# Tiles moved to multiples of 512 bytes, keys and values padded to five full pieces, five matmuls on zeros ahead of the first keys

## The chip, the cores and the metric

The kernel runs on one core of one Trainium2 chip. The metric is the device time of one execution in microseconds (us), the median over several runs.

## The reference

Linear attention over 4 batches of 576 tokens with 8 heads of 64, a normalisation, and then two gated layers of the same shape (512 to 1536 to 512) on all 2304 tokens, in float32:

```python
kv = np.einsum('bhsd,bhse->bhde', k, v)
out = np.einsum('bhsd,bhde->bhse', q, kv)
out = out / np.sqrt(np.mean(out * out, axis=-1, keepdims=True) + 1e-06) * g_norm
x = out.transpose(0, 2, 1, 3).reshape(2304, 512)
x = (x @ w_a) * (x @ w_b) @ w_out                       # first layer
x = 1.0 / (1.0 + np.exp(-(x @ w_gate))) * (x @ w_val) @ w_out2   # second layer
```

## The kernel before

**The layers.** Both layers are worked in twelve rounds: two layers (m) by six quarters of the hidden width (q). A round has three groups, one for each token tile j, whose two halves hold 256, 384 or 512 tokens (`NB`). The 512 by 512 blocks of a group are multiplied with seven block products instead of eight (names "1" to "7", in the order of `SLOTS`), each for the two hidden blocks u and v. Every operand is split into a high and a low part, so one block product is six matmuls: two slices of the contraction by high-high, high-low and low-high (line 724, in `product`). The stationary operand is a tile `wp0` to `wp3` with the weights ("1" and "2" use `wp0`, "5" and "7" use `wp1`, "6" and "4" use `wp2`, "3" uses `wp3`), the moving operand lies in `area0` or `area1`. The projection back to 512 ("down", line 837) uses `wo` and the gated values `gu`, `gv`. In the first round of a layer the moving operands are made on the chip (`x_comb`, line 477 and its neighbours) and stored to DRAM (line 481); in the later rounds they are loaded from there (line 496).

One round thus has 252 product matmuls (84 of each length; of the 84, 24 each on `wp0`, `wp1`, `wp2` and 12 on `wp3`) and 120 down matmuls (72 of 512 columns, 48 of 384).

**The attention.** `keys_values(b)` loads a batch's keys and values in four pieces (one for two heads), multiplies them with float32 matmuls of 128 columns (line 563), and ACT copies the diagonal blocks into `kvbd`. 576 rows are 4.5 times 128: four products use 128 partitions, and the fifth uses 64 partitions of a further piece `rest`, which holds the end of all four and is loaded first. Keys of batch 0 go to the arena, those of later batches to parts of `part0` to `part2` that are not yet in use (`PLACES`). Queries follow per token tile (line 639), then the squares, the mean and the root on ACT, DVE and POOL, a transpose on TensorE (line 674) and a copy into `part`. A float32 matmul leaves two records in the trace, a transposing one leaves one.

**The order.** A planner (`Plan.order`) plays the program with estimated costs and due times and writes one fixed order for every engine; the table `SHIFT` moves single due times. All DMAs are issued by SP, in that order: an issue that waits holds those behind it. Raw weights (line 345) are loaded into a ring of two buffers. Such a buffer is free once ACT (lines 354, 358) and DVE (`sign`, line 370) have read it.

**Places in SBUF.** Tiles are laid one after another, each rounded up to 32 bytes of a partition. `ident` has 512 bytes; `gcol` and `warm` have one word each, the two `ss`, the one `root` and the two `rr` buffers 96 bytes each. In the built program the tiles behind them start at these remainders of 512: `part0` to `part2` 160, both areas 192, `wp0` 192, `wp3` 384, `wp1`, `wp2`, `wo`, `gu` and `gv` 160. Offsets inside the tiles that line 724 and line 837 use are multiples of 512.

Of the kernel before, what the change touches and what calls it, by code (L numbers as in the profile page):

```python
# [23 lines left out]
P = 128  # L24
KC = DM // P
# [8 lines left out]
KJ = 4  # L34
LAST = S - KJ * P
# [19 lines left out]

STARTS = (24000, 50000, 75000)

SHIFT = {
# [26 lines left out]
}  # L85
ANY_ORDER = ("o0", "o1")
ARENA = ("xr",)
# [150 lines left out]
def attention_then_two_moes(  # L238
# [17 lines left out]
    gcol = one.tile([P, 1], F32, name="gcol")  # L256
# [15 lines left out]
    def new_tile(tag, shape, dtype=F32):  # L272
        if tag in ATTENTION:
            lo, n = ATTENTION[tag][0], int(np.prod(shape))
            i = turns[tag] = (turns.get(tag, -1) + 1) % RINGS.get(tag, 1)
            t = area(0)[:, lo + i * n:lo + (i + 1) * n]
            return t if len(shape) == 1 else t.rearrange("p (a b) -> p a b", a=shape[0])
# [34 lines left out]
    def mms(n):  # L312
        return 6 * (n / 2.4 + 9.5 + n / 90)
# [20 lines left out]
    FIRST = [("load", (0, c)) for c in "ab"] + [("kv", 0, p) for p in (KC, *range(KC))] + [("q", t) for t in range(4)]  # L334
    FIRST += ["gcol"] + [("load", (1, c)) for c in "ab"]
    FIRST += [("kv", 1, p) for p in (KC, *range(KC))] + [("q", t) for t in range(4, 9)]
    FIRST += [("kv", 2, p) for p in (KC, *range(KC))] + [("q", t) for t in range(9, 12)] + [("kv", 3, p) for p in (KC, *range(KC))]
# [188 lines left out]
    PLACES = [(2, 0, 0), (2, 0, LOADED), (2, 1, 0), (2, 1, LOADED), (1, 0, 0), (1, 1, 0)]  # L526
    PLACE_OF = {1: (0, 1, 2, 3, 4), 2: (5, 0, 1, 2, 3), 3: (0, 1, 2, 0, 3)}
# [6 lines left out]
    def keys_values(b):  # L534
        bank = ("K", b)
        rest = ("kv", b, KC)

        for p in (KC, *range(KC)):
# [373 lines left out]
    with tc.manual_schedule():  # L912
# [6 lines left out]
        for o in done:  # L919
            o["fn"](ENG[o["on"]]) if len(o["eng"]) == 2 else o["fn"]()  # L920
# [35 lines left out]
```

## Time and profile before

| | us |
|---|---|
| median of 3 runs | 934.97 (932.95 to 935.36) |
| the profiled execution, its own time | 928.55 |
| span of the profiled execution, first to last instruction | 926.8 |
| TensorE busy in it | 891.4 (96%) |
| VectorE / ScalarE / GpSimd busy | 626.3 / 404.1 / 417.1 |
| DMA | 255.66 MB, 276 GB/s |

The span and the execution's own time differ by 1.75 us, which lie around the span; the profiled execution was 6.4 us shorter than the median of the others. Busy time says how long an engine had something under way, not that it could not have been faster.

### The profile page before, as it was taken

Reading aid. Unit: us, or ns where it says so; the run is one execution under the profiler, and the core shown is the slowest. Engines: PE = TensorE matmul, PEld = TensorE weight load, DVE = VectorE, ACT = ScalarE, POOL = GpSimd, SP = SyncE. Lnnn points to the kernel's source line nnn. Section 1 sums busy time; section 2 is a strip of 40 time slices with the busy share of each in tenths; the row PEclk is TensorE's granted clock in tenths of the full one; section 3 lists DMA queues with packets and bytes.
Section 4 is the critical chain, followed back from the end, with each engine's and each line's share of the span. In section 5 each row is a group of like instructions: output and inputs, shape, how many; then the busy total and the mean of one; then the engine's idle time right before and its main releaser. Section 6 shows DMA issues by size and latency. Waiting matters only on the chain.

```text
span 926.8 us, 13401 instructions
## 1 busy us (share of the span) xinstructions
PE 891.4 (96%) x4856; PEld 798.5 (86%) x4856; DVE 626.3 (68%) x1082; ACT 404.1 (44%) x761; POOL 417.1 (45%) x387
## 2 busy tenths in 40 slices
PE   6798997999999999999999999999999999999998
PEld 5687886889988989989989988889989889989986
DVE  3577885378768866766769886767767677645445
ACT  3465653334344433343355555445444344333231
POOL 2568743265545415425458873345534414322111
PEclk9799999999999999999999999999999999999999
DMA  8896477988888797787694578798697696587573
GB/s 294 263 313 229 184 260 228 363 322 327 289 325 311 245 370 267 250 346 274 211 376 188 212 294 334 257 349 321 225 370 270 235 346 245 193 318 239 187 278 124
DMA packets 55472, 255.66 MB, mean 276 GB/s; under 512 B 6256, under 2 KB 8304, under 8 KB 44656
## 3 DMA queue, kind: packets, MB, share of 16 engines
q1 hardware_dynamic: 55408, 254.83, 75.0%
q8 instruction: 38, 0.62, 0.3%
q14 instruction: 26, 0.21, 0.1%
HBM read 217.06 MB, written 37.75 MB: 275 GB/s over the span
## 4 chain that ended last, share of the span: by engine, by line
PE 87%; DMA 7%; ACT 2%; DVE 2%; POOL 1%; issue 1%; SPq 0%; ACTq 0%; DVEq 0%; POOLq 0%
PE ps_u L724 53%; PE ps_o L837 29%; DMA raw<-w_all_dram 4%; PE ps_o L563 3%; PE ps_o L639 1%; DMA x<-area 1%; PE ps_o L674 1%; DMA area<-x 1%; DMA part<-kv_in_dram 1%; DMA area<-kv_in_dram 1%; ACT mag L354 0%; POOL wp L422 0%; DVE mag L370 0%; DVE gf L798 0%; POOL w L376 0%
## 5 line engine op out<-in xcount | busy, mean ns | idle before, releaser
L724 PE MATMUL ps_u<-area,wp 128*128 128x256 f32 (+2 forms) x3024 | 556.1, 339 | 13.0 <-DMA area<-x 4.7
L724 PEld LDWEIGHTS ps_u<-area,wp 128*128 128x128 f32 x3024 | 492.7, 189 | 62.9 <-ACT vu L326 5.1
L837 PE MATMUL ps_o<-gu,wo 128*128 128x512 f32 (+1 forms) x720 | 188.9, 370 | 1.8 <-DVE part L851 0.9
L837 PE MATMUL ps_o<-gv,wo 128*128 128x512 f32 (+1 forms) x720 | 187.3, 368 | 0.0
L847 DVE TENSOR_TENSOR part<-ps_o,part 128x512 f32<-128x512 f32 (+1 forms) x200 | 126.6, 635 | 84.0 <-PE ps_o L837 83.1
L376 POOL TENSOR_TENSOR w<-mag,last 128x512 int32<-128x512 int32 x72 | 96.5, 1345 | 127.9 <-DVE mag L370 119.8
L837 PEld LDWEIGHTS ps_o<-gv,wo 128*128 128x128 f32 x720 | 132.7, 188 | 17.6
L837 PEld LDWEIGHTS ps_o<-gu,wo 128*128 128x128 f32 x720 | 129.3, 188 | 19.4 <-DVE part L851 1.4
L806 POOL TENSOR_TENSOR gu<-gf,gu 128x512 fp32r<-128x512 f32 (+2 forms) x50 | 53.1, 1063 | 169.1 <-ACT gu L803 169.0
L354 ACT ACTIVATE mag<-raw 128x512 f32<-128x512 f32 x72 | 48.2, 669 | 75.0 <-DMA raw<-w_all_dram 63.7
L422 POOL TENSOR_TENSOR wp<-tmp,wp 128x512 fp32r<-128x512 f32 x33 | 43.6, 1321 | 75.9 <-ACT wp L418 75.9
L362 DVE TENSOR_SCALAR mag<-mag 128x512 f32<-128x512 f32 x72 | 36.6, 509 | 35.8 <-ACT mag L354 35.7
L803 ACT ACTIVATE gu<-gf 128x256 fp32r<-128x256 f32 (+2 forms) x72 | 37.5, 521 | 43.2 <-DVE gf L798 42.5
L370 DVE SCALAR_TENSOR_TENSOR mag<-raw,mag 128x512 uint32<-128x512 uint32 x72 | 49.4, 687 | 0.8
L418 ACT ACTIVATE wp<-tmp 128x512 fp32r<-128x512 f32 x48 | 30.3, 632 | 42.0 <-PE ps_u L724 34.2
L422 POOL TENSOR_TENSOR wp<-w,wp 128x256 fp32r<-128x256 f32 (+1 forms) x30 | 29.7, 991 | 41.8 <-ACT wp L418 41.6
L418 ACT ACTIVATE wp<-w 128x512 fp32r<-128x512 f32 (+1 forms) x48 | 25.2, 525 | 52.2 <-PE ps_u L724 41.3
L358 ACT ACTIVATE last<-raw 128x512 int32<-128x512 uint32 x72 | 47.5, 663 | 0.0
L326 ACT ACTIVATE u2u<-ps_u 128x512 f32<-128x512 f32 (+2 forms) x34 | 16.8, 494 | 69.3 <-PE ps_u L724 69.3
L806 POOL TENSOR_TENSOR gv<-gf,gv 128x384 fp32r<-128x384 f32 (+2 forms) x30 | 31.3, 1044 | 28.5 <-ACT gv L803 28.1
L803 ACT ACTIVATE gv<-gf 128x256 fp32r<-128x256 f32 (+2 forms) x72 | 37.7, 523 | 13.3 <-DVE gf L798 11.2
L806 DVE TENSOR_TENSOR gv<-gf,gv 128x256 fp32r<-128x256 f32 (+2 forms) x42 | 37.0, 880 | 8.9 <-ACT gv L803 8.9
(88 smaller groups left out, 892.6 us busy)
## 6 DMA issues: line engine op xcount, KB each, us to landing
area<-x SPq DMA_DIRECT2D x70, 1024.0 KB, 6.8
area<-x SPq DMA_DIRECT2D x70, 768.0 KB, 5.5
raw<-w_all_dram SPq DMA_DIRECT2D x72, 512.0 KB, 5.7
area<-x SPq DMA_DIRECT2D x70, 512.0 KB, 5.8
x<-area SPq DMA_DIRECT2D x14, 1024.0 KB, 4.7
x<-area SPq DMA_DIRECT2D x14, 768.0 KB, 3.3
x<-area SPq DMA_DIRECT2D x14, 512.0 KB, 4.0
part<-kv_in_dram SPq DMA_DIRECT2D x12, 512.0 KB, 5.7
```

The source lines that it names most:

```text
L354: A.activation(out=tl["mag", k], in_=words(1).bitcast(F32), func=ACTF.Abs, scale=65536.0)
L358: A.activation(out=tl["last", k], in_=words(0), func=ACTF.Copy, scale=2.0**-29)
L362: V.tensor_scalar(out=m, in0=m, scalar1=LEAST, scalar2=MOST, op0=ALU.max, op1=ALU.min)
L370: V.scalar_tensor_tensor(out=m, in0=words(1), scalar=0x80000000, in1=m, op0=ALU.bitwise_and, op1=ALU.bitwise_or)
L376: G.tensor_tensor(out=tl["w32", k].bitcast(I32), in0=tl["mag", k].bitcast(I32), in1=tl["last", k], op=ALU.add)
L418: A.activation(out=tl[name][:, 0, :], in_=tl[src][:, cut], func=ACTF.Copy)
L422: eng.tensor_tensor(out=t[:, 1, :], in0=tl[src][:, cut], in1=t[:, 0, :], op=ALU.subtract)
L724: nc.tensor.matmul(out=o, lhsT=wt[:, a, c], rhs=x[:, b, k, :], start=(i in "152" and k == 0 and (a, b) == (0, 0)), stop=(k == 1 and (a, b) ...
L803: A.activation(out=tl[whole][:, 0, c], in_=tl[me, "gf", t], func=ACTF.Copy)
L806: eng.tensor_tensor(out=tl[whole][:, 1, c], in0=tl[me, "gf", t], in1=tl[whole][:, 0, c], op=ALU.subtract)
L837: nc.tensor.matmul(out=o[:, :N], lhsT=tl["wo", f_of(g, uv)][:, a, c], rhs=tl[rhs["uv".index(uv)]][:, b, :], start=(uv, a, b) == ab[0], sto ...
L847: V.tensor_tensor(out=acc, in0=o, in1=acc, op=ALU.add)
```

## The change

Five edits. The small tiles (`gcol`, `warm`, `ss`, `root`, `rr`) become slices of one tile `small` of 896 bytes, so that in the built program every tile behind it starts at a multiple of 512 bytes. Keys and values are padded with zero rows from 576 to 640, so that a batch has four pieces of five times 128 rows and no `rest`; there are five places for them. Five float32 matmuls of 512 columns on the zeroed `kvbd[1]` stand ahead of everything else on TensorE. The planner's cost of six matmuls has another formula. `SHIFT` is another table.

```diff
-KJ = 4
-LAST = S - KJ * P
+KJ = 5
+HEAT = 5
...
 ANY_ORDER = ("o0", "o1")
+SMALL = {"ss": 32, "root": 32 + 6 * H, "rr": 32 + 9 * H}
+SMALL_WORDS = 224
...
     ident = one.tile([P, P], F32, name="ident")
-    gcol = one.tile([P, 1], F32, name="gcol")
+    small = one.tile([P, SMALL_WORDS], F32, name="small")
+    gcol, warm = small[:, 0:1], small[:, 1:2]
...
     def new_tile(tag, shape, dtype=F32):
+        if tag in SMALL:
+            i = turns[tag] = (turns.get(tag, -1) + 1) % RINGS.get(tag, 1)
+            t = small[:, SMALL[tag] + i * 3 * H:SMALL[tag] + (i + 1) * 3 * H]
+            return t if len(shape) == 1 else t.rearrange("p (a h) -> p a h", a=3)
...
     def mms(n):
-        return 6 * (n / 2.4 + 9.5 + n / 90)
+        return 6 * (n + 16 * -(-n // 256)) / 2.4
...
-    PLACES = [(2, 0, 0), (2, 0, LOADED), (2, 1, 0), (2, 1, LOADED), (1, 0, 0), (1, 1, 0)]
-    PLACE_OF = {1: (0, 1, 2, 3, 4), 2: (5, 0, 1, 2, 3), 3: (0, 1, 2, 0, 3)}
+    PLACES = [(2, 0), (2, LOADED), (2, 2 * LOADED), (1, 0), (1, LOADED)]
+    PLACE_OF = {1: (0, 1, 2, 3), 2: (4, 0, 1, 2), 3: (0, 1, 2, 0)}
...
-                for j, t in enumerate([tl[kv][:, j] for j in range(KJ)] + [tl[rest][:, p]]):
-                    nc.tensor.matmul(out=tl[bank][:, p, :], lhsT=t[:, 0, :], rhs=t[:, 1, :], start=(j == 0), stop=(j == KJ))
+                t = tl[kv]
+                for j in range(KJ):
+                    nc.tensor.matmul(
+                        out=tl[bank][:, p, :], lhsT=t[:, j, 0, :], rhs=t[:, j, 1, :], start=(j == 0), stop=(j == KJ - 1)
+                    )
...
         V.memset(kvbd[1], 0.0)
         G.memset(kvbd[0], 0.0)
+        hot = bank_of("o0")
+        for _ in range(HEAT):
+            nc.tensor.matmul(out=hot, lhsT=kvbd[1][:, 0, :], rhs=kvbd[1].rearrange("p k n -> p (k n)"), start=True, stop=True)
...
-    kv_in = np.zeros((B, KC + 1, P, KJ, 2, P), np.float32)
-    kv_in[:, :KC] = kv[:, :, :KJ * P].reshape(B, KC, P, KJ, 2, P)
-    kv_in[:, KC, :LAST] = kv[:, :, KJ * P:].transpose(0, 2, 1, 3, 4)
-    kv_in = kv_in.reshape(B, KC + 1, P, KJ * 2 * P)
+    kv_in = np.zeros((B, KC, P * KJ, 2, P), np.float32)
+    kv_in[:, :, :S] = kv
+    kv_in = kv_in.reshape(B, KC, P, KJ * 2 * P)
```

The start of TensorE's order, before: keys of batch 0 (`area_92`), queries of the first four token tiles (`ps_u`), keys of batch 1 (`part_67`, and `part_66` for the `rest`).

```order
L563 MATMUL ps_o_115<-area_92 128x128 x20
L639 MATMUL ps_u_151<-area_71,part_65 128x128 x4
L639 MATMUL ps_u_160<-area_71,part_65 128x128 x4
L639 MATMUL ps_u_167<-area_71,part_65 128x128 x4
L639 MATMUL ps_u_194<-area_71,part_65 128x128 x4
L563 MATMUL ps_o_221<-part_67 128x128 x4
L563 MATMUL ps_o_221<-part_66 128x128
```

The same place in the changed kernel:

```order
L932 MATMUL ps_o_82<-area_71 128x512 x5
L573 MATMUL ps_o_125<-area_98 128x128 x20
L650 MATMUL ps_u_191<-area_71,part_65 128x128 x4
L650 MATMUL ps_u_197<-area_71,part_65 128x128 x4
L650 MATMUL ps_u_205<-area_71,part_65 128x128 x4
L650 MATMUL ps_u_219<-area_71,part_65 128x128 x4
L573 MATMUL ps_o_241<-part_67 128x128 x15
L573 MATMUL ps_o_241<-part_66 128x128 x5
```

The five matmuls on zeros stand first; what follows has kept its order, with three pieces of batch 1 in `part_67` and one in `part_66`.

The start of SP's order of DMA issues, before: raw weights (`raw`), queries (`part_65`, `area_71`), keys and values of batch 0 (`area_92`) and batch 1 (`part_66`, `part_67`).

```order
L345 DMA raw<-w_all_dram 128x512
L632 DMA part_65<-q_t_dram 128x512
L556 DMA area_92<-kv_in_dram 64x1024
L556 DMA area_92<-kv_in_dram 128x1024 x4
L632 DMA part_65<-q_t_dram 128x512 x2
L345 DMA raw<-w_all_dram 128x512 x2
L556 DMA part_66<-kv_in_dram 64x1024
L556 DMA part_67<-kv_in_dram 128x1024
L632 DMA part_65<-q_t_dram 128x512
L556 DMA part_67<-kv_in_dram 128x1024
L345 DMA raw<-w_all_dram 128x512
L865 DMA gcol<-g_col_dram 128x1
```

In the changed kernel:

```order
L357 DMA raw<-w_all_dram 128x512 x2
L565 DMA area_98<-kv_in_dram 128x1280 x4
L643 DMA part_65<-q_t_dram 128x512 x3
L357 DMA raw<-w_all_dram 128x512
L565 DMA part_67<-kv_in_dram 128x1280
L643 DMA part_65<-q_t_dram 128x512
L357 DMA raw<-w_all_dram 128x512
L565 DMA part_67<-kv_in_dram 128x1280
L877 DMA small<-g_col_dram 128x1
L565 DMA part_67<-kv_in_dram 128x1280
L565 DMA part_66<-kv_in_dram 128x1280
```

Two raw loads now stand ahead of the first keys, each piece of keys is 640 KB instead of 512 KB, and the last piece of batch 1 stands behind the fourth raw load, as two of its pieces did before.

## Rows read from the trace of the kernel before

**Rows 1.** The page: the span, busy time of each engine.
```profile
span 926.8 us, 13401 instructions
...
PE 891.4 (96%) x4856; PEld 798.5 (86%) x4856; DVE 626.3 (68%) x1082; ACT 404.1 (44%) x761; POOL 417.1 (45%) x387
```

**Rows 2.** Stretches: length, then each engine's busy us, granted clock, DMA share, GB/s.
```profile
core 0: us, PE busy (x) PEld busy (x) DVE busy (x) ACT busy (x) POOL busy (x), PEclk, DMA share, GB/s
0.00:5.00 5.00, 0.00 (x0) 0.00 (x0) 0.79 (x2) 2.48 (x4) 1.18 (x8) 1.00 0.63 210
...
10.00:15.00 5.00, 5.00 (x23) 4.09 (x21) 0.00 (x0) 0.00 (x0) 0.00 (x0) 1.00 1.05 391
...
20.00:25.00 5.00, 4.06 (x32) 3.50 (x30) 4.42 (x9) 3.10 (x7) 3.76 (x8) 1.00 0.69 133
...
30.00:35.00 5.00, 4.14 (x16) 3.07 (x16) 1.29 (x2) 0.76 (x2) 2.77 (x4) 0.50 0.59 202
...
40.00:50.00 10.00, 9.14 (x68) 8.03 (x67) 8.15 (x16) 6.80 (x15) 5.79 (x10) 1.00 0.92 312
...
200.00:923.00 723.00, 719.21 (x3864) 647.85 (x3862) 497.69 (x864) 303.27 (x573) 311.29 (x259) 1.00 0.76 279
```

**Rows 3.** The same view, inside and over one steady round.
```profile
289.35:290.78 1.43, 1.43 (x13) 1.42 (x12) 1.43 (x3) 0.71 (x2) 1.43 (x3) 1.00 0.72 221
290.78:292.19 1.41, 1.41 (x14) 1.41 (x13) 0.76 (x2) 1.24 (x3) 1.41 (x2) 1.00 0.89 259
308.81:310.17 1.36, 1.36 (x14) 1.36 (x12) 1.36 (x4) 0.78 (x2) 1.25 (x2) 1.00 0.68 262
...
312.25:314.37 2.12, 2.12 (x13) 2.12 (x13) 1.92 (x3) 2.10 (x5) 2.12 (x2) 1.00 0.87 294
330.34:333.10 2.76, 2.76 (x13) 2.25 (x13) 2.56 (x6) 1.42 (x3) 1.05 (x2) 1.00 0.87 289
335.89:338.62 2.73, 2.73 (x13) 2.25 (x12) 0.69 (x1) 0.63 (x1) 0.46 (x1) 1.00 1.01 402
286.61:355.41 68.80, 68.80 (x374) 62.22 (x374) 51.30 (x93) 29.23 (x54) 30.09 (x28) 1.00 0.84 308
```

**Rows 4.** Timeline of TensorE in that round: start, us, engine, line, operation.
```profile
338.62 0.68 PE L837 MATMUL ps_o<-gu,wo 128*128 128x384 f32 x3
...
340.70 2.96 PE L724 MATMUL ps_u<-area,wp 128*128 128x512 f32 x12
343.50 0.70 PE L837 MATMUL ps_o<-gu,wo 128*128 128x384 f32 x3
```

**Rows 5.** Timeline, the first 41 us.
```profile
0.89 0.48 DVE L917 MEMSET area<- 128x512 f32 x1 [0.89 <-PEq L945]
...
7.50 9.04 PE L563 MATMUL ps_o<-area 128*128 128x128 f32 x40 [7.50 <-DMA area<-kv_in_dram]
...
40.31 1.57 PE L563 MATMUL ps_o<-part 128*128 128x128 f32 x10
```

**Rows 6.** Chain that ended last, in order of time, the first 34 us.
```profile
19.84 0.69 DVE mag L370
...
20.59 0.33 SPq L345
...
21.44 6.14 DMA part<-kv_in_dram
...
27.62 5.49 PE ps_o L563 x20
```

**Rows 7.** The same chain from 142 us on.
```profile
143.06 9.35 DMA x<-area
...
152.79 6.68 DMA area<-x
```

**Rows 8.** Who waited for whom: engine, line, releaser, us, times, longest.
```profile
PE ps_u L724 <- DMA area<-x: 4.7, 4, 2.4
...
PE ps_o L563 <- DMA part<-kv_in_dram: 3.6, 1, 3.6
```

More of the change, by code (lines that the diff above doesn't have):

```diff
@@ L330, in move @@
             eng.tensor_scalar(out=out, in0=in_, scalar1=scale, scalar2=None, op0=ALU.mult)
-    FIRST = [("load", (0, c)) for c in "ab"] + [("kv", 0, p) for p in (KC, *range(KC))] + [("q", t) for t in range(4)]
+    FIRST = [("load", (0, c)) for c in "ab"] + [("kv", 0, p) for p in range(KC)] + [("q", t) for t in range(4)]
     FIRST += ["gcol"] + [("load", (1, c)) for c in "ab"]
-    FIRST += [("kv", 1, p) for p in (KC, *range(KC))] + [("q", t) for t in range(4, 9)]
-    FIRST += [("kv", 2, p) for p in (KC, *range(KC))] + [("q", t) for t in range(9, 12)] + [("kv", 3, p) for p in (KC, *range(KC))]
+    FIRST += [("kv", 1, p) for p in range(KC)] + [("q", t) for t in range(4, 9)]
+    FIRST += [("kv", 2, p) for p in range(KC)] + [("q", t) for t in range(9, 12)] + [("kv", 3, p) for p in range(KC)]
     load_due = {name: 100 * i - 1e5 for i, name in enumerate(FIRST)}
@@ L535, in keys_values @@
         bank = ("K", b)
-        rest = ("kv", b, KC)
-        for p in (KC, *range(KC)):
+        for p in range(KC):
             kv = ("kv", b, p)
@@ L545, in keys_values @@
                 before, new, uses = last_in.get(place, []), [], []
-                last_in[place] = [("K", b, x) for x in (range(KC) if p == KC else (p,))]
+                last_in[place] = [("K", b, p)]
             def load(p=p, kv=kv):
-                rows = P if p < KC else LAST
                 if b == 0:
@@ L552, in load @@
                 else:
-                    j, h, lo = PLACES[PLACE_OF[b][p]]
-                    t = part[j][:, h].rearrange("p k n -> p (k n)")[:, lo:lo + LOADED]
-                t = t[:rows]
-                nc.sync.dma_start(out=t, in_=kv_in[b, p, :rows])
+                    j, lo = PLACES[PLACE_OF[b][p]]
+                    t = part[j].rearrange("p h k n -> p (h k n)")[:, lo:lo + LOADED]
+                nc.sync.dma_start(out=t, in_=kv_in[b, p])
                 tl[kv] = t.rearrange("p (j c e) -> p j c e", c=2, e=P)
@@ L561, in mm @@
                     tl[bank] = bank_of("o1").rearrange("p (k n) -> p k n", k=KC)
-                for j, t in enumerate([tl[kv][:, j] for j in range(KJ)] + [tl[rest][:, p]]):
-                    nc.tensor.matmul(out=tl[bank][:, p, :], lhsT=t[:, 0, :], rhs=t[:, 1, :], start=(j == 0), stop=(j == KJ))
-            op(kv, "SP", dma(512 if p < KC else 256), load, before, new, rank=load_due[kv], lag=2000)
-            if p < KC:
-                op(("K", b, p), "PE", 1130, mm, [kv, rest] + ([("K", b, p - 1)] if p else [("O", t) for t in tiles_of.get(b - 2, ())]),
-                   [] if p else [("o1", bank)], ([bank] if p else []) + (uses + [rest] if b == 0 else []))
+                t = tl[kv]
[3 more added lines that the diff above has]
+                    )
+            op(kv, "SP", dma(640), load, before, new, rank=load_due[kv], lag=2000)
+            op(("K", b, p), "PE", 1130, mm, [kv] + ([("K", b, p - 1)] if p else [("O", t) for t in tiles_of.get(b - 2, ())]),
+               [] if p else [("o1", bank)], ([bank] if p else []) + uses)
         prior = ("K", b, KC - 1)
@@ L606, in newton @@
             m, y = flat(tl[ss][:, :n, :]), tl["root", lot]
-            tl[rr] = new_tile("rr", [3, H, 1])
+            tl[rr] = new_tile("rr", [3, H]).rearrange("p a (h o) -> p a h o", o=1)
             r = tl[rr][:, :n].rearrange("p a h o -> p (a h o)")
@@ L697, in queries @@
         op(tbank, "PE", 450, transpose, [xn], [("o1", tbank)], [xn, "attention"])
-        free = [k for j, h, *_ in pieces(t) for i, x in enumerate(PLACES) if x[:2] == (j, h) for k in last_in[i]] if t >= NQ0 else [("O", i) for i in range(NQ0)]
+        free = [k for j, h, *_ in pieces(t) for i, (J, lo) in enumerate(PLACES)
+                if J == j and lo < (h + 1) * KC * NB[j] and h * KC * NB[j] < lo + LOADED for k in last_in[i]] if t >= NQ0 else [("O", i) for i in range(NQ0)]
         op(("Y", t), MOVE, {"ACT": 435 + 190 * len(pieces(t)), "DVE": 520 + 160 * len(pieces(t))}, to_x, [tbank, "gcol"] + free, uses=[tbank])
@@ L912, in attention_then_two_moes @@
     with tc.manual_schedule():
-        warm = one.tile([P, 1], F32, name="warm")
         G.memset(warm, 0.0)
```

56 rows, old and new, of the table SHIFT are left out of this document.

## The prediction

> **What bounds the kernel now.** I read the page first: TensorE is busy for 891.4 of 926.8 us and no other engine for more than 626.3 [rows 1]. Busy does not say whether its matmuls could follow each other faster, so I went on to the stretches. From 200 us to the end of the last matmul TensorE is busy 719.21 of 723 us at the full clock [rows 2]: there only the spacing of its matmuls counts. Before 200 us idle time counts, and the chain and the waits say what it waits for.
>
> The spacing first. Rows 3 cut one round at the first matmul of a weights tile. A stretch also counts the matmuls still under way at its edges; twelve start in each, so the spacing is the length over twelve. The moving tile lies in an area all through, at remainder 192. With 256 columns twelve matmuls take 1.43 us on `wp0` (119.2 ns each), 1.41 on `wp1` (117.5) and 1.36 on `wp3` (113.3) [rows 3]. With 384 columns `wp1` takes 2.12 us (176.7) [rows 3], twelve down matmuls 2.08 (338.62 to 340.70, 173.3) [rows 4]. With 512 columns `wp2` takes 2.80 (340.70 to 343.50, 233.3) [rows 4], `wp0` 2.76 and 2.73 (230.0 and 227.5) [rows 3]. Same engine, same clock, same length and moving area: what differs is the stationary tile, and with it its place. So each length has a floor (113.3, 173.3, 227.5) that some pairs of tiles reach and others miss by 3 to 6 ns. The whole round, 286.61 to 355.41, takes 68.80 us without idle time [rows 3].
>
> The start next. TensorE waits 7.50 us for the first keys, and the 40 records of batch 0 take 9.04 us, 0.226 each [rows 5]. Ten such records take 1.57 at the full clock [rows 2, 5], 0.157 each, and twenty take 5.49 while the granted clock is 0.50, that is 1.2 GHz [rows 2, 6], 0.275 each. So the first 40 run mostly at the lower level: 0.275n + 0.157(40 - n) = 9.04 gives n = 23, and 6.4 us of work before the clock rose. Then TensorE waits 3.6 us for keys of batch 1 [rows 8]. The chain shows why they are late: DVE's `sign` at 19.84 freed a raw buffer, SP could issue the raw load at 20.59, and only behind it, at 21.44, the keys [rows 6]. DMA moved 391 GB/s from 10 to 15 us, but 133 from 20 to 25 [rows 2]. The wait also costs clock, since the 5.49 us follow it.
>
> **The change, part by part.** The starts at 512. If every pair reaches the floor, a round takes 84 x (113.3 + 173.3 + 227.5) + 72 x 227.5 + 48 x 173.3 ns = 67.9 us instead of 68.80; twelve rounds give **-10.9 us**. That is the one end. No row shows both tiles at remainder 0. The nearest rows are pairs with one common remainder: `wp0` and the area, both 192, and `wo` with `gu` or `gv`, both 160. They reach the floor with 384 columns [rows 4], nearly reach it with 512 (228.8 in the mean of 2.76 and 2.73), but need 119.2 with 256 [rows 3]. If these rows hold for all pairs, a round takes 84 x (119.2 + 173.3 + 228.8) + 72 x 228.8 + 48 x 173.3 ns = 68.6 us, and twelve rounds give -2.6. I take the floor: a 512-byte row of weights at remainder 160, 192 or 384 lies across two pieces of 512 bytes and at 0 in one, and the moving row touches one piece less; a common remainder alone keeps both crossings. Since `wp3` shows 113.3 even with a crossing, nothing in 256 columns forbids it. Steady rounds have cover for this: VectorE is busy 51.30 and GpSimd 30.09 of 68.80 us, and DMA 0.84 [rows 3], so 1.3% less per round starves none of them.
>
> A rule speaks against this term. The Trainium skill, "TensorE: Matmul & The Clock Gate", Part 2, says that TensorE reads the moving and the stationary operand through two independent ports, so that loading the next weights takes nothing from the running matmul; by that alone the place of a tile would change nothing and this term would be 0. The spacings by weights tile in rows 3 speak against reading it so.
>
> The five matmuls on zeros. They wait for DVE's memset, over at 0.89 + 0.48 = 1.37 us [rows 5]. Ten records of four times 128 columns cost at most four times 0.275 or 0.157, so 1.10 or 0.63 us. With the clock rising after 6.4 us of work, six records run at the lower level and four at the upper: 8.9 us, over at 10.3. If they cost only what one pass of 512 columns does (2 x 0.228 at the lower level, [rows 3]), they are over at 5.9; if the clock stays low, at 12.4. I take 10.3. The first keys then take 40 x 0.157 = 6.3 and end at 16.6, as before (7.50 + 9.04 = 16.5). Bounds: with 5.9 the keys' own loads set the pace. Two raw loads and four pieces are 3.7 MB; with 1.05 MB moved in the first 5 us and 391 GB/s then [rows 2] the last lands near 12, so the keys end near 14 (-2.5). With 12.4 and the low clock for all, 12.4 + 11.0 = 23.4 (+6.9). The cover is the wait for the first keys; what is left over delays only this batch, because batch 1 waits for its loads.
>
> The order of the loads. Up to the last piece of batch 1 the new order moves four raw loads, eight pieces and four queries: 2.1 + 5.2 + 1.05 = 8.4 MB, so it lands at 5 + (8.4 - 1.05)/0.391 = 24 us if SP is not held. The third raw load needs the first buffer and the fourth the second; in the built order ACT now reads both raw tiles ahead of the keys' diagonal, whereas before the second stood behind it. So the hold at 19.84 goes, batch 1 ends 1.6 us after its last piece, near 26 to 27 instead of 27.62 + 5.49 = 33.1 [rows 6]: **-6**. Late next are the other batches: their padding is 0.5 MB more, at 391 GB/s 1.3 us. The fuller matmul for the fifth piece costs TensorE nothing, since 64 partitions ran as a matmul of its own already. Of the 4.7 us left I hold back 0.7 for the stage up to 200 us, whose order is new throughout: **-4**, bounds -8 (with the -2.5 above) and 0 (a later wait takes all of it).
>
> The small tiles in one tile keep their slices apart, so they add no wait in the built order; the planner's formula acts through the order alone. Sum: -10.9 - 4 = -15: span 912, own time 913.5. The profiled execution (928.55) lies 6.4 us below the median, so I set the same change against 934.97: **920 us**.
>
> **Rivals.** (a) The common remainder sets the spacing, 256 columns need 119.2 everywhere: -2.6 - 4, about 928. For it: the rows of `wp0`. Against it: the floor at the other two lengths and on `wp3`.
>
> (b) Places do not matter, and the differences come from something else that goes with the weights tile: 0 - 4, about 931. Against it: in rows 3 length, moving area and clock are the same, and nothing else in them differs with the weights tile. This is what the rule of the Trainium skill above ("TensorE: Matmul & The Clock Gate", Part 2) makes of the change.
>
> (c) The zeros do not raise the clock, the edit does not do what it says: then batch 0 ends 6.9 us later, and since TensorE works in order, this eats the 4 gained at batch 1 and leaves 2.9: -10.9 + 2.9, about 927. For it: they are zeros, and no row shows work on zeros. Against it: the granted clock follows how busy TensorE was in all rows here (0.50 after the wait, full after work [rows 2, 5]).
>
> (d) Slower. In the first rounds an operand is stored and loaded again through SP's one queue. The chain holds one such pass at 143.06: 9.35 us for the store, 6.68 for the load [rows 7], 16 us, of which TensorE waited 4.7 in all [rows 8]. The new order interleaves stores, loads and raw loads differently. If two passes stand bare, each costs up to 16 - 4.7 = 11.3 us more: +22.6 - 15, about 943. It decides from the second bare pass; one leaves 931. For it: the queue is held by one raw load already now [rows 6]. Against it: DMA has room, 279 GB/s on average after 200 us against 391 at best [rows 2].
>
> **How the numbers follow.** Forecast 62% (its own range 912 to 925), (a) 13%, (b) 7%, (c) 9%, (d) 9%. The range, 8 in 10, reaches from 907 (both terms at their best end give 934.97 - 10.9 - 8 = 916; TensorE is idle for 200 - (891.4 - 719.2) = 28 us before 200 us [rows 1, 2], and the new order may remove 9 of what the terms don't count) to 931, which takes in (a), (b) and (c) and leaves (d) out. About 0.3% either way, 932.2 to 937.8, is what a measurement of this kernel can tell from no change. The forecast and (c) are faster, (a) nearly always, (b) mostly; (d) is slower: faster 0.86, same 0.07, slower 0.07.
>
> **What would show it.** In the profile after: a steady round of 67.9 us, and 1.36, 2.08 and 2.73 us for twelve matmuls on every weights tile; 1.43 on all tiles with 256 columns means (a), unchanged differences (b). At the start: ten records on zeros from 1.4 to about 10 us, the first keys at 0.157 a record (0.275 means (c)), the end of batch 1 at 26 to 27 us, and no raw load between its pieces on the chain. I am wrong above all if the waits for loaded operands between 60 and 200 us grow, or if the spacing does not move.

## The result, and the profile after

The changed kernel takes **906.96 us** at the median (906.26 to 907.38, 4 runs); the kernel before took 934.10 beside it (932.95 to 935.36, 4 runs). The ratio is 0.9708, its 95% interval 0.9692 to 0.9725. That is 27 us less where I had forecast 15, and it ends 0.04 us below the range. The two profiled executions differ by less, 21.5 us in their spans, because the one of before was 6.4 us shorter than the median.

The page of the profiled execution (own time 907.14), to be held against [rows 1]; the last row is the clock in 40 slices (9 says 90% or more; the mean over the execution is 0.999):

```profile
span 905.3 us, 13421 instructions
...
PE 882.7 (98%) x4866; PEld 793.4 (88%) x4866; DVE 618.4 (68%) x1071; ACT 402.9 (45%) x759; POOL 425.2 (47%) x400
...
PEclk9999999999999999999999999999999999999999
```

Ten more records, yet 8.7 us less busy: the clock is full from the first keys to the last matmul, and no stretch in between runs at 0.50 as in [rows 2, 6].

The stretches that answer to [rows 2, 3], columns as there. The second to fourth are twelve matmuls of 256 columns on `wp0`, `wp1` and `wp3`, the fifth of 384 on `wp1`, the sixth of 512 on `wp0`, the seventh the same steady round:

```profile
20.00:25.00 5.00, 3.56 (x32) 3.59 (x33) 4.59 (x9) 3.00 (x7) 2.51 (x9) 1.00 0.96 362
267.94:269.38 1.44, 1.44 (x14) 1.43 (x13) 1.43 (x4) 0.63 (x1) 1.11 (x2) 1.00 0.25 43
269.38:270.81 1.43, 1.43 (x14) 1.43 (x13) 1.43 (x4) 0.91 (x2) 0.85 (x1) 1.00 0.82 292
287.54:288.98 1.44, 1.44 (x14) 1.43 (x13) 1.44 (x3) 0.79 (x2) 1.33 (x2) 1.00 0.60 233
291.06:293.14 2.08, 2.08 (x13) 2.08 (x13) 2.06 (x5) 1.08 (x3) 0.74 (x1) 1.00 0.36 121
309.12:311.88 2.76, 2.76 (x14) 2.25 (x14) 2.34 (x6) 2.52 (x6) 1.62 (x2) 1.00 0.86 315
267.94:336.78 68.84, 68.84 (x373) 62.39 (x372) 50.43 (x95) 27.60 (x52) 32.03 (x29) 1.00 0.84 311
```

The steady round takes 68.84 us; it took 68.80 [rows 3]. So nothing came from the round. With 256 columns every weights tile now shows 1.43 to 1.44, `wp3` too, which had 1.36 [rows 3]. `wp1` with 384 columns went from 2.12 to 2.08.

The timeline of TensorE over the first 28 us, which answers to [rows 5, 6] (L932 zeros, L573 keys):

```profile
1.43 7.04 PE L932 MATMUL ps_o<-area 128*128 128x512 f32 x10 [1.43 <-DVE area L928]
8.56 1.38 PE L573 MATMUL ps_o<-area 128*128 128x128 f32 x10
10.10 2.91 PE L573 MATMUL ps_o<-area 128*128 128x128 f32 x20 [0.16 <-DMA area<-kv_in_dram]
13.17 1.38 PE L573 MATMUL ps_o<-area 128*128 128x128 f32 x10 [0.17 <-DMA area<-kv_in_dram]
...
21.44 4.70 PE L573 MATMUL ps_o<-part 128*128 128x128 f32 x40 [1.70 <-DMA part<-kv_in_dram]
```

Zeros end at 8.47, the first keys at 14.55, batch 1 at 26.14. The waits that answer to [rows 8], in the same columns:

```profile
PE ps_o L573 <- DMA part<-kv_in_dram: 1.7, 1, 1.7
...
PE ps_u L736 <- DMA area<-x: 1.0, 1, 1.0
```

Where the time comes from is read from the start of the same matmul in both timelines; the 3024 product matmuls are numbered as they run. Number 1 starts at 34.12 (before 41.81, 7.7 us earlier), number 337 at 150.47 (168.14, 17.7), number 505 at 198.94 (219.23, 20.3), number 2269 at 683.90 (704.07, 20.2), the last at 890.19 (911.81, 21.6). Nearly the whole gain is made in the first 200 us; behind them the two kernels run almost alike.

### The profile page after: what moved, and what is told of

It reads as the page before. It is cut to its first block, busy times and chain, and to the rows that moved or that the text cites. A ratio compares the mean times of both kernels' runs of the same rounds, so it can differ in the third digit from the quotient of the medians.

```text
span 905.3 us, 13421 instructions
## 1 busy us (share of the span) xinstructions
PE 882.7 (98%) x4866; PEld 793.4 (88%) x4866; DVE 618.4 (68%) x1071; ACT 402.9 (45%) x759; POOL 425.2 (47%) x400
## 4 chain that ended last, share of the span: by engine, by line
PE 90%; DMA 5%; ACT 2%; DVE 1%; POOL 1%; issue 0%; SPq 0%; ACTq 0%; POOLq 0%
PE ps_u L736 55%; PE ps_o L849 31%; PE ps_o L573 1%; DMA raw<-w_all_dram 1%; PE ps_o L650 1%; DMA area<-kv_in_dram 1%; DMA part<-kv_in_dram 1%; DMA area<-x 1%; PE ps_o L685 1%; DMA area<-q_t_dram 1%; ACT part L338 1%; POOL s L467 0%; ACT last L370 0%; DVE area L340 0%; DVE part L859 0%
## 5 line engine op out<-in xcount | busy, mean ns | idle before, releaser
L736 PE MATMUL ps_u<-area,wp 128*128 128x256 f32 (+2 forms) x3024 | 550.5, 337 | 4.0 <-ACT vu L338 1.2
L818 POOL TENSOR_TENSOR gu<-gf,gu 128x512 fp32r<-128x512 f32 (+2 forms) x52 | 55.2, 1061 | 168.8 <-ACT gu L815 168.8
L382 DVE SCALAR_TENSOR_TENSOR mag<-raw,mag 128x512 uint32<-128x512 uint32 x72 | 52.5, 733 | 0.7
L818 POOL TENSOR_TENSOR gv<-gf,gv 128x384 fp32r<-128x384 f32 (+2 forms) x36 | 38.5, 1070 | 15.0 <-ACT gv L815 14.9
L338 ACT ACTIVATE vu<-ps_u 128x384 f32<-128x384 f32 (+2 forms) x44 | 21.4, 485 | 52.4 <-PE ps_u L736 43.9
L338 ACT ACTIVATE u2u<-ps_u 128x384 f32<-128x384 f32 (+2 forms) x32 | 15.9, 496 | 59.0 <-PE ps_u L736 58.9
```

What stands on the lines that cost most here:

```text
L338: A.activation(out=out, in_=in_, func=ACTF.Copy, **({} if scale is None else {"scale": scale}))
L382: V.scalar_tensor_tensor(out=m, in0=words(1), scalar=0x80000000, in1=m, op0=ALU.bitwise_and, op1=ALU.bitwise_or)
L736: nc.tensor.matmul(out=o, lhsT=wt[:, a, c], rhs=x[:, b, k, :], start=(i in "152" and k == 0 and (a, b) == (0, 0)), stop=(k == 1 and (a, b) ...
L818: eng.tensor_tensor(out=tl[whole][:, 1, c], in0=tl[me, "gf", t], in1=tl[whole][:, 0, c], op=ALU.subtract)
```

## The experiments

Times are medians; ratios are to the kernel before, run beside each, whose median lay between 931.91 and 934.85. A gain or loss given in us behind a ratio is that ratio's difference times 934. "New code" is the changed kernel's code, "new order" the row that its planner wrote for each engine. Code cuts are shortened.

### The places of the tiles

`PADS` gives the bytes of an unused tile that is laid ahead of the tile named.

```diff
+PADS = {'part': 160, 'area0': 32, 'wp3': 192, 'wp1': 288}   # old remainders in the new code
+PADS = {'area0': 320, 'wp0': 192}                            # areas at 320, all else at 0
+PADS = {'area0': 192, 'wp0': 192}                            # areas at 192, all weights at 384
```

> The changed kernel, order and all, with its tiles put back on the remainders of before by unused tiles between them (parts 160, areas and wp0 192, wp3 384, wp1, wp2, wo, gu and gv 160). The order theory: the places are worth nothing in sum, the time stays at 907 (905 to 909), and the spacing of matmuls with 256 columns goes back from 120 ns on all weights tiles to 119, 117 and 113. The places theory: the remainder 0 brought part of the gain, so 912 or more.

Measured: 907.50 us (905.06 to 908.35), ratio 0.9715 [0.9688, 0.9741]. The new places are worth nothing in sum. The old spacing came back with the old remainders: twelve matmuls of 256 columns on `wp3`, and the steady round, in this run:

```profile
287.06:288.42 1.36, 1.36 (x14) 1.36 (x12) 1.30 (x3) 0.78 (x2) 1.14 (x1) 1.00 0.79 330
267.60:336.40 68.80, 68.80 (x373) 62.23 (x372) 49.90 (x95) 28.05 (x54) 32.12 (x30) 1.00 0.85 315
```

So the spacing does go with the places, `wp3`'s 1.36 too; only the sum over a round hardly moves.

> The changed kernel with the areas (the moving operands) at remainder 320 and all weights tiles still at 0, so that the stationary row begins 192 behind the moving one, as wp3 did before. If the distance between the two remainders sets the spacing: 256 columns at 113 to 114 instead of 120, 384 and 512 unchanged, 6 to 7 us less than the changed kernel. If what counts is whether a row crosses a multiple of 512: the moving rows cross now, and all three lengths get slower than with 0.

Measured: 904.72, in one run, which by itself tells nothing of 2 us. Twelve matmuls of 256 columns on `wp3` took 1.42 us there, 118 ns each, and not the 113 to 114 of the theory.

> The changed kernel with the areas of the combinations at remainder 192 and all weights at 384, which is the pair of remainders that the tile wp3 had in the kernel of before; nothing else is changed. Theory (it is the two remainders themselves that set the spacing): products of 256 columns come at 113.5 ns instead of 119.5 (909 of them: 5.4 us), 384 and 512 columns as they are, so 901.5 us, 899 to 904. Rival (wp3's 113 ns came from something else than its place): 120 ns again and 906 to 908 us.

Measured: 903.73 (901.41 to 907.27, 6 runs), ratio 0.9669 [0.9631, 0.9708]. Twelve matmuls of 256 columns on `wp0` and on `wp3`, and the round, in its stretches:

```profile
266.99:268.40 1.41, 1.41 (x13) 1.41 (x12) 1.40 (x4) 0.63 (x1) 1.14 (x3) 1.00 0.16 48
286.49:287.91 1.42, 1.42 (x13) 1.41 (x12) 1.42 (x3) 0.79 (x2) 1.27 (x2) 1.00 0.70 280
...
266.99:335.63 68.64, 68.64 (x374) 62.18 (x372) 50.55 (x95) 27.53 (x52) 32.12 (x30) 1.00 0.85 315
```

118 ns instead of 120, so the place does count a little: 0.2 us a round, some 2.4 us in twelve. But `wp3`'s 113 ns did not come back with `wp3`'s two remainders; that half of my theory fell: it takes the places of all the tiles, as in the first run of this section, and which of them matters is open.

### The zeros

```diff
-HEAT = 5
+HEAT = 0
```

> The changed kernel without the five matmuls on zeros. The order theory: the keys of batch 0 begin near 7.5 us and run at the lower clock, 0.23 to 0.275 a record instead of 0.15, and end near 16 to 17 instead of 14.6; 2 us of that reach the end, so 909 (908 to 911), the clock stays up later. The zeros theory: they keep the clock up through the whole start, without them it falls once or twice more, 913 or more. If the wait for the keys of batch 1 hides it: 907.

Measured: 906.09 (903.82 to 907.09), ratio 0.9701 [0.9669, 0.9732]. Without zeros the first keys start as they land, at 7.13, take 6.28 us instead of 5.99 and end at 13.41, sooner than with them (14.55): the zeros run on until 8.47, when the keys are there already. From 7.13 to 10.40 only 15 records are under way (0.22 us each), from 10.40 to 13.41 there are 27 (0.11 each), so the first keys do run slower without zeros; it costs nothing at the end.

### The padding

```diff
+                    r = 64 if j == KJ - 1 else P
-                        ... lhsT=t[:, j, 0, :], rhs=t[:, j, 1, :] ...
+                        ... lhsT=t[:r, j, 0, :], rhs=t[:r, j, 1, :] ...
```

> The changed kernel with the fifth matmul of each key product on 64 partitions again (it leaves out the rows on the other 64). The padding theory, formed from the profile after: a weights load on 64 partitions between loads on 128 stops TensorE, so a key product of ten records takes 1.49 instead of 1.17 us, 0.3 us times 16 products: 911 (909 to 912.5). The rival, and my prediction: the height costs nothing, 907.

This kernel leaves out rows of the keys and values, so only its time is read. Measured: 911.20 (909.67 to 914.28), ratio 0.9777 [0.9740, 0.9813]: 6.4 us lost at 934. The weight loads of its batch 1, and the stretch that they begin in:

```profile
21.28 1.76 PEld L574 LDWEIGHTS ps_o<-part 128*128 128x128 f32 x8 [1.86 <-issue]
23.26 0.50 PEld L574 LDWEIGHTS ps_o<-part 64*128 64x128 f32 x2 [0.23 <-issue]
23.98 1.78 PEld L574 LDWEIGHTS ps_o<-part 128*128 128x128 f32 x8 [0.22 <-issue]
...
21.31:25.00 3.69, 3.69 (x15) 3.24 (x15) 3.31 (x8) 1.54 (x5) 2.26 (x7) 0.50 0.84 335
```

Ahead of and behind the weight loads of 64 rows the loads stand still for 0.22 to 0.23 us here, but the clock was at 0.50 in this stretch. At the full clock it is about half of that: the old code in the new order (o2, below) idles 1.0 us in all ahead of the 64-row loads of eight products, and ten records take 1.47 us there against 1.28 in the changed kernel. Two of the runs without the padding had a mean clock of 1.000 and took 909.67 and 910.00: 3 us more than the changed kernel by the times as they stand, 5 by the ratio to the kernel beside them. So 3 to 5 of the 6 us are the height alone.

The other way round, in the kernel before (the fifth piece padded to 128 partitions):

```diff
-                t = t[:rows]
-                nc.sync.dma_start(out=t, in_=kv_in[b, p, :rows])
+                nc.sync.dma_start(out=t, in_=kv_in[b, p])
```

> The kernel before with the fifth piece (the rest) loaded and multiplied on 128 partitions, its lower half zeros, and 256 KB more to load for each batch; order unchanged. The padding theory: ten records of keys in 1.17 to 1.3 us instead of 1.49, 3 to 5 us less: 929 to 931. The rival: DMA pays for it, 934 or more.

Measured: 926.01 (924.29 to 931.14, 10 runs), ratio 0.9942 [0.9921, 0.9964], 5.4 us gained.

### Single moves in the order of before

`place` moves one operation in the planner's finished list.

```diff
+    place(("load", (1, "b")), after=("kv", 1, 3))             # e7: raw load behind the keys
+        place(("xd", (0, 0, 2), i), before=("xh", (0, 1, 0), "7"))   # e8: stores 7 and 3 first
```

> The kernel before with one DMA issue moved: the fourth raw load stands behind the last two pieces of batch 1 instead of ahead of them. The order theory: TensorE's wait of 3.6 us at 24 to 27.6 goes, batch 1 no longer runs at the lower clock and ends near 27 instead of 33.1, and 4 to 6 us reach the end: 928 to 930. The rival: the DMA queue is full anyway and later waits take it back: 933 to 935.

Measured: 927.36 (923.10 to 930.06), ratio 0.9926 [0.9896, 0.9957], 6.9 us gained; the wait ahead of batch 1 is gone (22.60 to 28.58).

> The kernel before with two DMA issues moved: the last two stores of the first round stand ahead of the loads that wait for room. The order theory: the waits for loaded operands between 143 and 160 us (4.7 us) and the fall of the clock behind them go: 928 to 931. The rival: the loads wait for room whatever stands between them, and the time stays: 933 to 935.

Measured: 929.71 (925.63 to 934.63, 10 runs), ratio 0.9962 [0.9933, 0.9991], 3.5 us gained, but not by the way that I expected: the longest wait on `area<-x` is still 3.1 us.

> The kernel before with the raw load behind the keys, the two stores ahead of the loads, and the rest on 128 partitions. If the three gains add: 934 - 7 - 4.5 - 4 = 918 (915 to 921), half or more of the whole gain. If they are one gain seen three times: 925 or more.

Measured: 921.51 (918.23 to 923.85), ratio 0.9881 [0.9843, 0.9919]: 11 of the 27 us. The single gains, 5.4, 6.9 and 3.5, do not quite add up, and more than half was still to be found.

### Whole orders exchanged

```diff
-    done = plan.order()
+    plan.order()
+    done = [plan.by[name] for name in LISTED]   # the other kernel's row, with its engines and x places
```

The new code in the old order (o1):

> The changed kernel's code (tiles at multiples of 512 bytes, keys padded to five full pieces, zeros), but every engine's instructions in the order of before, on the engines that before gave them to, and the x tiles at before's places; the loads of the rests, which the new code lacks, are left out of that order. Theory (the new order brings what places, zeros and padding by themselves don't, and those three were worth 0, 0 and about 4.5 us): 929 us, 926 to 932, with a hold of the keys of batch 1 behind the raw load, low stretches of the clock and waits on area<-x as in before. Rival (the gain is mostly the padding's, through the four loads that go, and the order is worth little): 915 or less. Second rival (both are needed and neither alone gives more than a few us): 932 here and more than 925 for the kernel of before in the new order.

The old code in the new order (o2):

> The kernel of before (old places, rest loads of 64 rows, no zeros) with every engine's instructions in the changed kernel's order, on its engines, the x tiles at its places; the load of a batch's rest stands just ahead of the batch's first keys (for batch 3 where its place comes free). Theory (order worth some 22 us): 912 us, 908 to 916, with the clock at full from the first keys on. Rival (the order is worth little): 925 or more.

Measured: o1 925.48 (923.89 to 928.81, 9 runs), ratio 0.9911 [0.9885, 0.9937]; o2 907.90 (905.89 to 911.16), 0.9722 [0.9677, 0.9767]. The order alone gives 26 of the 27 us, the code alone 8, and with the new order in place the code adds about 1, which the intervals do not tell from 0. The theory stands, with sizes a little off: the two end 0.5 and 0.1 us below the ranges I gave them.

One thing in o2 is not as I described it: its tiles are not at the old places. A pool of tiles is laid when the row first asks for it, so in the old code a new order moves the tiles behind the small ones too. Its steady round, and twelve matmuls of 256 columns on `wp3`:

```profile
270.32:338.80 68.48, 68.48 (x374) 62.22 (x372) 50.01 (x95) 27.57 (x52) 32.58 (x30) 1.00 0.84 316
...
289.87:291.30 1.43, 1.43 (x14) 1.43 (x13) 1.34 (x3) 0.78 (x2) 1.21 (x1) 1.00 0.59 239
```

68.48 us is 0.36 less than the changed kernel's round and 0.32 less than that of before. Over twelve rounds that is an estimated 4 us, and it hides most of what the padding brings: number 505 starts at 201.72 in o2, 2.8 us later than in the changed kernel, and the last of the 3024 at 889.13, 1.1 us earlier. So some 22 of the 26 us are the order itself, and some 4 are places that came with it.

Then the seam: new order to a point, old order behind it (h1 to 50 us, h3 to 105), and the reverse (h4). An x tile for which the place in its row was taken got another that was free.

> The changed kernel's code; all engines in the new order up to the first pair of blocks' product u7 (the first 50 us or so), and what is left in the order of before. Theory (the loss of the old order is spread: about a third in the start, a third at 70 to 80 us, a third at 110 to 160 us): 920 us, 917 to 923, with the low stretches near 80 and 160 us still there. Rival (the start holds all): 909 or less. Second rival (the start holds nothing, since padding and zeros already mend it): 925.

> As the run before, with the seam later: new order up to the product u5 of the third block (the first 105 us or so), old order behind it. Theory: the wait of 2.3 us on POOL's lower half near 75 us and the low stretch behind it go as well, and what is left is the wait on the x tiles near 155 us with its low stretch and the downs that come late: 914 us, 911 to 917. Rival (the last part, 105 to 180 us, holds most): 919 or more. Second rival (it holds nothing): 908.

> The changed kernel's code, all engines in the order of before up to the product u5 of the third block (some 105 us) and in the new order behind it: the reverse of the run with the new order to 105. Theory (the stretch behind 105 us holds 14 us by itself): 912 us, 908 to 915, with the low stretch near 75 us still there and none behind it. Rival (the late part is only good behind the early part, which leaves the x tiles and downs ready in time): 919 or more.

Measured: h1 927.32 (0.9936 [0.9905, 0.9966]), h3 920.78 (0.9879 [0.9843, 0.9915]), h4 914.73 (0.9794 [0.9762, 0.9826]). From o1 over h1 and h3 to the changed kernel the ratio goes 0.9911, 0.9936, 0.9879, 0.9708: nothing from the first 50 us, 5 us from there to 105, 16 us behind 105. The first two steps are no larger than the width of their intervals; o1 to h3, the first 105 us together, is 3. By the reverse the last part gives 11 alone, and the first 105 us then give 8. My "a third each" was wrong; the larger part lies behind 105 us.

Stretches of 50 to 105 and 105 to 200 us, first of the new code in the old order:

```profile
50.00:105.00 55.00, 50.80 (x343) 47.91 (x343) 44.45 (x76) 34.09 (x66) 41.61 (x56) 0.94 0.69 251
105.00:200.00 95.00, 86.19 (x434) 73.72 (x433) 62.25 (x102) 40.49 (x74) 41.04 (x34) 0.98 0.75 277
```

and of the changed kernel:

```profile
50.00:105.00 55.00, 49.18 (x329) 45.00 (x328) 43.76 (x76) 34.66 (x65) 41.89 (x52) 1.00 0.70 257
105.00:200.00 95.00, 92.25 (x483) 81.60 (x482) 66.34 (x115) 46.33 (x83) 44.08 (x37) 1.00 0.84 324
```

Behind 105 us TensorE is busy 6 us more, and the queue moves 324 GB/s instead of 277. What holds the queue is in its own waits, 100 to 175 us (us, times, longest). Old order in the new code:

```profile
SPq L3875 <- DMA x<-area: 29.0, 4, 8.9
```

The changed kernel:

```profile
SPq L508 <- PE ps_u L736: 27.6, 12, 7.3
...
SPq L508 <- DMA x<-area: 12.6, 2, 11.6
```

In the old order SyncE stands 29 us, four times, on loads of x tiles whose own stores have not landed, and everything in its row stands behind them. In the new order the stores come earlier, two such waits are left, and the largest sum is now for room that TensorE's own products free. TensorE waits for x tiles 1.0 us in this kernel and 4.4 in o1. All waits of the queue in this stretch add up to about the same, 66 us in o1 and 64 in the changed kernel: what differs is what it waits for. The other runs fall on the two sides as their rows say: h3, with the old row there, stands 28.7 us on such loads, four times; h4 and o2, with the new one, 11.3 and 12.1, twice.

### SyncE's row by itself

```diff
     one stretch of SyncE's row in the changed kernel (xd: store, xh: load of an x tile), by before's order
-    xd7 xh1 xd3 xh5 xh2 xh6 xh7 xh4 xh3 xd4
+    xh1 xh5 xh2 xh6 xd4 xh7 xh4 xd7 xh3 ... xd3     # k1 also takes the raw load (3, b) behind xh4
```

> The changed kernel with one stretch of SyncE's row as in before: the stores of x tiles 4, 7 and 3 of the third block, the loads of the x tiles of the next pass's first two blocks and one raw load in the order that before has; every other engine as in the changed kernel. Theory A (SyncE's row decides): TensorE waits again for x tiles near 135 and 155 us, 2 to 4 us each, with a low stretch of the clock behind them: 916 us or more. Theory B (TensorE's row decides, the down products between the first products cover the loads whatever their row): 907 to 910.

Measured: 921.81 (919.49 to 925.45), ratio 0.9878 [0.9842, 0.9913]. This is theory A's number, but not its mechanism. The waits of 125 to 145 us:

```profile
ACT mag L3733 <- DMA raw<-w_all_dram: 14.4, 1, 14.4
...
PE ps_o L4216 <- ACT gv L4182: 11.5, 1, 11.5
```

ScalarE's new row has the work on that raw weight early; with the load at its old, late place ScalarE stands on it for 14.4 us, the gate `gv` stands behind that, and TensorE waits 11.5 us. On x tiles it waits 1.2 in the whole run. So this run shows what two rows cost that do not fit each other, and not what the stores cost.

> The changed kernel with the stores of the third block's x tiles and the loads of the next pass's x tiles in the order of before, the raw load among them left at its new place; every other engine as in the changed kernel. Theory (stores that stand behind blocked loads make TensorE wait for x tiles, as in before at 155 us): waits on x tiles of 3 to 5 us in all between 130 and 165 us, 911 us, 909 to 914. Rival (the down products between the first products cover the loads, and what the late part of the old order loses lies in the rows of the computing engines): 907 to 908.5.

Measured: 912.13 (911.88 to 913.59), ratio 0.9768 [0.9707, 0.9829], some 5 us lost, as the theory had it. The interval just reaches the changed kernel's 0.9708, but all four runs lie above that kernel's four (906.26 to 907.38). SyncE's own waits from 100 to 175 us, and TensorE's from 130 to 200:

```profile
SPq L3875 <- DMA x<-area: 25.6, 5, 8.5
```

```profile
PE ps_u L4103 <- DMA area<-x: 2.1, 2, 1.5
PE ps_u L4103 <- DVE u2v L3707: 2.0, 1, 2.0
```

The waits of the old row are back in the queue, and a third to a half of what the late part holds is back in the time. TensorE's waits on x tiles grew by only 1.1 us, less than the 3 to 5 that I expected; 2.0 more are a wait on a copy by VectorE. From number 253 to number 337 this run takes 26.48 us (126.79 to 153.27), the changed kernel 22.85 (127.62 to 150.47), so most of the loss is made there.

### The clock

```diff
+    def fill(out, times):
+        for _ in range(times):
+            nc.tensor.matmul(out=out, lhsT=ident, rhs=ident, start=True, stop=True)
...
+                    if b == 1:
+                        fill(tl[bank][:, 0, :], 14)
...
+            fill(o[:, :P], FILL.get((g, uv, i), 0))     # 9 ahead of two products
```

> The kernel of before, order and tiles as they are, with matmuls on the identity into a bank that is overwritten behind them, at three places where TensorE waits: 14 ahead of the keys of batch 1 (about 3.3 us), 9 each (about 2.1 us) ahead of the product u1 of the second block and of the second block of the next pass. The waits stay, filled. Theory (the low stretches of the clock follow TensorE's long waits and cost as much as these): the low stretches near 28, 82 and 160 us go, 17 us at half clock in the profiled run, so 8 us faster, 926 us at the median, 923 to 929, and the scatter of 928 to 940 narrows. Rival (the clock falls by something else, or the fillers come late themselves): 933 or more.

Measured: 932.82 (928.83 to 938.34, 12 runs), ratio 1.0008 [0.9982, 1.0033]. The clock did rise: its mean was 0.994 to 0.998 in these runs and 0.985 to 0.994 in the 23 of before, and one low stretch of 3.4 us was left in the profile. The time stayed. The first product came 3.8 us earlier (38.05), product 1261 only 0.3 (427.04 against 427.37), and the last matmul 0.5 later. Its waits show where the lead went: less on x tiles than in [rows 8], more on ScalarE's copies (`vu`), whose four waits lie behind 200 us in both. First the kernel before, then this run:

```profile
PE ps_u L724 <- ACT vu L326: 3.8, 4, 1.3
PE ps_u L724 <- POOL area L477: 2.3, 1, 2.3
PE ps_u L724 <- ACT u2u L326: 1.3, 1, 1.3
...
PE ps_u L732 <- ACT vu L331: 6.5, 4, 1.8
PE ps_u L732 <- POOL area L482: 2.0, 1, 2.0
PE ps_u L732 <- ACT u2u L331: 1.8, 1, 1.8
...
PE ps_u L732 <- DMA area<-x: 1.4, 2, 1.1
```

So the theory that the low stretches cost as much again as the waits fell, since a gain of 8 us lies well outside the interval. At number 505 the lead is still 2.7 us (216.54 against 219.23), and the waits on `vu` grew by the same 2.7: with the order as it is, a faster TensorE arrives earlier at the next thing that is not ready.

### Joined

New code and order, no zeros, areas at remainder 320 (`HEAT = 0`, `PADS = {'area0': 320, 'wp0': 192}`).

> The changed kernel without the zeros and with the areas of the combinations at remainder 320, all else at 0. Expected from the single changes: zeros 0 to -1, areas 1.5 us less: 905 us, 903 to 906.5. Rival (both were scatter): 907.

Measured: 903.91 (902.76 to 907.88, 5 runs), ratio 0.9708 [0.9674, 0.9741]. The median is 3 us lower than the changed kernel's, the ratio is the same to the fourth digit: no gain that these runs can tell.

## Why the prediction was wrong

**The starts at 512 (-10.9).** This step failed: "I take the floor: a 512-byte row of weights at remainder 160, 192 or 384 lies across two pieces of 512 bytes". It measured 0. A crossing of 512 bytes is not what sets the spacing: with all tiles at remainder 0, where no row crosses, every weights tile shows 1.43 to 1.44 us with 256 columns, and with the old crossings back `wp3` shows 1.36 again. The row that I set aside, the pair at one common remainder with 119.2 ns at 256 columns, was the one that held (rival (a)); its -2.6 was not there either, since what `wp1` won at 384 columns, for instance, `wp3` lost at 256. The rule of the Trainium skill that I had weighed ("TensorE: Matmul & The Clock Gate", Part 2, two independent read ports) gave the right sum, 0, for this change. The traces agree with it only so far: places do move single pairs by a few ns (120 at remainder 0, 118 at 192 apart), and the steady round by up to 0.36 us (68.84 against 68.48 in o2).

**The zeros.** They were over at 8.47 instead of 10.3, and the first keys do run at the full clock (1.38 for ten records), so rival (c) fell. I had put them at nothing, and they are worth nothing. I had the right reason, the wait for the first keys, but the keys land before the zeros end. One reading of mine needs a word: the profile's clock column says 1.00 from the start of the span, also where I took the first keys to run at the lower level [rows 2]; the level there is read from the spacing of the records alone.

**The order of the loads (-4).** Batch 1 ends at 26.14 where I had said 26 to 27: the step is right. Its worth by itself is that of the single move in before, 6.9, near my -6. As a stretch of the whole it gave nothing: the new order to 50 us and the old one behind it took as long as the old order throughout, so what was won at the start was lost again behind it.

**The fifth piece.** "The fuller matmul for the fifth piece costs TensorE nothing, since 64 partitions ran as a matmul of its own already" was mis-sized: I put the height of the fifth piece at 0, and the padding measured 5.4 us in the old order and 6.4 in the new, 3 to 5 of these at the full clock. Weight loads that stand still around a load of 64 rows go with it. With the whole old code in the new order only 1 us of it shows, in the main because that kernel's rounds are shorter by the places that its tiles got (68.48 us, some 4 in twelve rounds).

**The rest of the order.** This is where the 27 us lie, and the step that failed is "I hold back 0.7 for the stage up to 200 us, whose order is new throughout". I treated a new order as a risk of 0.7 us and named its gain only as a reason for the range's low end ("may remove 9"). It measured some 22 us by itself, 16 (or 11, by the reverse) behind 105 us. Part of the mechanism was in my own rival (d), store and load of an x tile through one queue, with the sign turned: the old order has four such passes standing in SyncE's row in that stretch and the new order two. I had looked at what TensorE waited for x tiles, 4.7 us [rows 8], only as something that a worse order could add to, and gave its removal no term. The queue's own waits in the kernel before, over the whole execution, would have said more:

```profile
SPq L496 <- DMA x<-area: 33.5, 5, 8.9
```

28.0 of the 33.5 us lie between 100 and 175 us, in four waits.

What stays open: how the late part's 11 to 16 us divide. SyncE's row by itself costs 5; the remainder must lie in the rows of the other engines or in how they fit that one, which was not taken apart. Nor was it tested which of the two edits to the planner, the cost formula or the table `SHIFT`, wrote the better order. And `wp3`'s 113 ns go with the places, but which tile's place makes them is not shown.

## What to carry to other kernels

When a change writes a new order for a queue, read that queue's own waits by what they wait for: here a load that stood on its own store held all that was behind it, while the waits for room that the bottleneck was about to free left it only 1.0 us of waiting for x tiles. Price two edits apart by exchanging them (old order in new code, new order in old code): the small edits that the change was named for gave 1 us, the order that came with them 26. Look, too, whether the exchange has moved something else: here it moved tiles, and with them some 4 us. And do not count a lead at one place as a gain at the end until nothing behind it is late: filling the waits raised the clock, brought the first product 3.8 us forward, and moved the end by nothing.

## What the runs showed of the hardware that I had not expected

- A float32 weight load of 64 rows between loads of 128 left the loads standing 0.22 to 0.23 us on either side with the clock at 0.50, and about 0.12 us ahead of it at the full clock (1.0 us over eight products in o2):

```profile
L3934 PEld LDWEIGHTS ps_o<-part 64*128 64x128 f32 x16 | 2.4, 184 | 1.0
```

- Matmuls of 256 columns follow each other in 120 ns with both tiles at remainder 0 and in 118 with the remainders 192 apart; the pair that showed 113 before shows 118 when all weights lie there, and 113 again when all tiles lie as before.
- The low stretches of the clock came behind the longest idle times of TensorE. In the new code with the old order TensorE idled 2.26 us, then the clock was at half speed:

```profile
73.38:75.64 2.26, 0.00 (x1) 0.00 (x0) 1.53 (x3) 0.61 (x2) 2.26 (x3) 0.82 0.41 120
75.64:81.60 5.96, 5.96 (x19) 5.96 (x20) 5.19 (x5) 2.52 (x4) 5.38 (x7) 0.50 0.65 267
```

In the new order TensorE's longest idle time behind the first keys was 1.70 us, and the clock stayed full. The length of the idle time does not settle it alone: the kernel with the fifth matmul on 64 partitions idled 1.70 us as well and then ran at 0.50 (21.31 to 25.00 us), while the last run of SyncE's row idled 2.0 us and kept a mean clock of 1.000. Filling the idle times in the kernel before bought nothing (above): there the low clock went with the waits and was not what set the end.
